# Broadcast loads of 1/den in a linear-attention block: 128 partitions in rows of 2 KB in place of 32 partitions in rows of 8 KB

## Chip, cores and metric

The kernel runs on one core of a Trainium2 chip. The metric is the device time of one execution in microseconds (us), lower is better. The core has five engines that the program gives separate instruction streams: PE (TensorE, matrix multiply), ACT (ScalarE), DVE (VectorE), POOL (GpSimd) and SP (SyncE). SP does no arithmetic here; it issues nearly all of the kernel's DMAs, in program order, and 16 DMA engines carry them out. A DMA tells of its landing by raising a semaphore by 16.

## Reference

One block of a conditioned transformer, all inputs and the output in bf16: S = 2048 tokens of width D = 1024, 32 attention heads of width 32, a feed-forward layer of width F = 3584.

```
mod = (silu(c) @ w_mod)                      # six vectors: sa, ca, ga, sb, cb, gb
h   = layernorm(x) * (1 + ca) + sa
q, k, v = heads of (h @ wqkv)
pq, pk  = phi(q), phi(k)                     # phi(t) = (t + 1 if t > 0 else exp(t)) + 1e-6
kv  = sum over s of pk[s, d] * v[s, e]       # per head
z   = sum over s of pk[s, d]
num = pq @ kv
den = (pq . z) + 1e-6                        # one number per head and token
x   = x + ga * ((num / den) @ wo)
h   = layernorm(x) * (1 + cb) + sb
x   = x + gb * ((gelu(h @ w_gate) * (h @ w_up)) @ w_down)
```

The part that matters here is the division by den.

## The kernel before

The kernel has one program, written out by a Python planner: every operation is recorded with the bytes it reads and writes, from which the waits follow, and each engine's stream is then emitted in the recorded order. In one stretch (from `mark[0]`, L1050, to L1765) a list scheduler, `reorder`, moves the DVE, ACT and POOL operations by estimated costs and due times; PE and SP keep the recorded order there. The loads of 1/den for token blocks 0 to 2, and the scaling of block 0 and of half of block 2, are recorded in that stretch, the rest behind it.

**Tiling.** Tokens are 16 chunks of 128 (`c_`), or 4 blocks of 512 (`sg`, 0 to 3), each block in two halves of `HW` = 256 tokens (`h`). The 32 heads are 8 groups (`g`, `NG` = 8) of 4 (`k`, `HPG` = 4); a group's 4 heads of width 32 fill the 128 partitions, so head k of a group lies in partitions 32k to 32k+31. `PQ[sg]` holds phi(q) as [128 partitions, 8 groups, 512 tokens].

**The path of 1/den.** `den` (L1235) makes the denominators of two blocks on PE (128 rows: block, half, head k, group g; 256 tokens along the row), takes their reciprocal on DVE and stores the 128 rows of 1 KB in DRAM, in `scr_rd[sg, h, k, g, t]` (L1248). `rb_load(sg, hs)` (L1255) brings them back, each head's values copied into the 32 partitions of that head: `RB[i]`, i = sg % 2, is [128, 2 halves, 8 groups, 256 tokens] in f32. For each block and half it issues four loads of 256 KB on SP's queue, one per head k: 32 partitions, each the same row of 8 KB. There are 32 such loads. `pq_scale(sg, h, gs)` (L1268) then multiplies phi(q) by RB on DVE, in four instructions per block and half, each over two head groups [128 x 512]; each of these waits for all four loads of its block and half (`rb_ops`).

**What uses it.** `wo_mm` (L1278) multiplies the scaled `PQ[sg]` of one chunk of 128 tokens by `W2` (K-V state times output weights) on PE, 16 matrix multiplies per chunk, and DVE adds the result to x (`x1`, L1291). A chunk can only be finished when both its block's half has been scaled and W2 is there.

**Order.** Around the change SP issues, in this order: the store of den 0; a transposing DMA `mT4` (L703); the 8 loads of block 0; `mT5` (PE needs it for `kv_prod(5)`, L913); the store of den 1; `mT6`; a small store of `mrg`; `mT7`; 16 loads (block 2 half 0, block 1 halves 0 and 1, block 2 half 1); then, between transposing DMAs `T2` of the second layer norm (`h2a`, `h2b`), loads of x and the first feed-forward weights `wt`, four loads for block 3 half 0 and four for half 1. Transfers on SP's queue take eight semaphores in turn ("lanes"): before SP issues a DMA, the DMA issued eight earlier must have landed. DVE and PE too run strictly in their order. Behind L1765 the chunks 3 to 13 of `wo_mm` come one after another, with the `pq_scale` of later blocks recorded between them (`SLOT`, L1769), and then the feed-forward layer: unit 0 (with chunks 14 and 15 inside it), and 27 more.

Of the kernel before, what the change touches and what calls it, by code (L numbers as in the profile page):

```python
# [10 lines left out]
P = 128  # L11
# [7 lines left out]
NG = 8  # L19
HPG = 4  # L20
# [310 lines left out]
def bass_adaLN_cond__linear_attn_block__geglu_ffn__prompt_kernel(  # L331
# [17 lines left out]
    scr_rd = nc.dram_tensor("scr_rd", [NSG, 2, HPG, NG, SGW // 2], f32).ap()  # L349
    with ExitStack() as es:  # L350
# [6 lines left out]
        def at(name, shape, dty, off):  # L357
            return nc.alloc_sbuf_tensor_at(name, shape, dty, offset=ABASE + off, align_bytes=4)
# [39 lines left out]
        RB = [at(f"rb{i}", [P, 2, NG, SGW // 2], f32, OFF_RB[i]) for i in range(2)]  # L398
# [46 lines left out]
        def r_sm(name):  # L445
            return [(SMO[name], SMO[name] + SMSZ[name], name)]
# [30 lines left out]
        def r_wv(g):  # L477
            return [(OFF_WK + g * 2048, OFF_WK + (g + 1) * 2048, "wv")]
# [4 lines left out]
        def r_pq(sg, k0=0, k1=NG, s0=0, s1=SGW):  # L483
            return r_t8(PQO[sg], f"pq{sg}", k0, k1, s0, s1)
# [46 lines left out]
        def r_rb(i, h, g0=0, g1=NG):  # L531
            return [(OFF_RB[i] + (h * NG + g0) * 1024, OFF_RB[i] + (h * NG + g1) * 1024, f"rb{i}")]
# [10 lines left out]
        def pr(b):  # L543
            return [(b * 2048, (b + 1) * 2048)]
# [7 lines left out]
        sch = Sched()  # L552
        T, A, V, G, Q = PE_, ACT_, DVE_, POOL_, SP_
# [64 lines left out]
        for q in range(1, 4):  # L618
            wmq_dma(q)
            for d0, d1 in ((2 * q, 2 * q + 1), (2 * q + 1, 2 * q + 2)):  # L620
# [8 lines left out]
               rd=r_sm("c8") + r_sm("ident"), pwr=pr(4))  # L629
# [4 lines left out]
               rd=r_sm("thc") + r_sm("chalf"), wr=r_sm("siluT"))  # L634
# [507 lines left out]
        for c_ in range(10, NCH):  # L1142
            b = seq.index(("k", c_ // 2 * 2, 0)) - (9 if c_ % 2 else 12)
# [6 lines left out]
        for c_ in range(8, NCH, 2):  # L1150
            b = seq.index(("k", c_, 0)) - 3
# [10 lines left out]
        for g in range(NG):  # L1162
            task(nk + g // 2, lambda g=g: sch.dma(Q, lambda e: e.dma_start(WV[:, g, :, :], wqkv_v[:, :, 2 * D + g * P:2 * D + (g + 1) * P]),
                                                  wr=r_wv(g), note=f"wv{g}"))
# [68 lines left out]
        HW = SGW // 2  # L1233
# [16 lines left out]
            return store  # L1250

        o_rd = {}
        rb_ops = {}

        def rb_load(sg, hs=(0, 1)):  # L1255
            i = sg % 2
            for h in hs:
                made = []
                for k in range(HPG):
                    made.append(sch.dma(Q, lambda e, h=h, k=k: e.dma_start(  # L1260
                        RB[i][32 * k:32 * (k + 1), h, :, :].rearrange("p a b -> p (a b)"),
                        scr_rd[sg, h, k:k + 1, :, :].rearrange("k g t -> k (g t)").to_broadcast([32, NG * HW])),
                        wr=r_rb(i, h) if k == 0 else (), deps=made[0].deps if k else [o_rd[sg // 2]], note=f"rb{sg}.{h}.{k}"))
                rb_ops[sg, h] = made

        GH = [((0, 2), (2, 4)), ((4, 6), (6, 8))]

        def pq_scale(sg, h, gs):  # L1268
            i, t0 = sg % 2, h * HW
            for g0, g1 in gs:  # L1270
                ap = PQ[sg][:, g0:g1, t0:t0 + HW]
                rng = r_pq(sg, g0, g1, t0, t0 + HW)
                sch.op(V, lambda e, ap=ap, i=i, h=h, g0=g0, g1=g1: e.tensor_tensor(ap, ap, RB[i][:, h, g0:g1, :], ALU.mult),
                       rd=rng + r_rb(i, h, g0, g1), wr=rng, deps=rb_ops[sg, h], note=f"pqs{sg}.{h}.{g0}")

        x1_ops, s_ops = {}, {}

# [28 lines left out]
        def hook_run(f):  # L1306
            if f[:2] == "kv":
                kv_prod(int(f[2:]), 4)
            elif f == "ga":
                ga_pass()  # L1310
            elif f == "gbr":
                assert mdone[0] == 64
                gb_rows()
            elif f == "modp":
                mod_pass()
            elif f == "z32":
                z32()
            elif f[:3] == "den":
                st[int(f[3:])] = den(int(f[3:]), 5)
                st[int(f[3:])]()  # L1320
            elif f[:2] == "ps":
                pq_scale(int(f[2]), int(f[4]), GH[0] + GH[1])
            elif f[:2] == "rb":
                rb_load(int(f[2]), (int(f[4]),))
            elif f[0] == "w":
                w2_pair(int(f[1:]))
# [27 lines left out]
        kv_prod(7, 5)  # L1354
        wo_mm(0, 0, [4, 5])
        rb_load(1)
        rb_load(2, (1,))
        w2_pair(3)
        wo_mm(1, 2, [3, 4, 5])
# [229 lines left out]
        def down(c_, k, b, c0, c1, fcs, last, after):  # L1589
# [5 lines left out]
            if last:  # L1595
                pset_writer(b, o)

        pq_scale(2, 0, GH[0] + GH[1])

        def r_wh(q, r, cc, name, j0, j1):  # L1600
# [165 lines left out]
        def cb1():  # L1766
            sch.op(V, lambda e: e.tensor_scalar(CB1T[:, :], CBT[:, :], 1.0, None, op0=ALU.add), rd=r_sm("cbT"), wr=r_sm("cb1T"))

        SLOT = {2: lambda: (pq_scale(1, 0, GH[0] + GH[1]), x_dma(NXR, 10)),  # L1769
                3: lambda: pq_scale(1, 1, GH[0] + GH[1]),  # L1770
                4: lambda: (cb1(), wt_dma(0)),
# [54 lines left out]
        for n in range(12):  # L1826
            q, i = divmod(n, 4)
# [6 lines left out]
        for u in range(2 * NFP):  # L1834
# [5 lines left out]
            else:  # L1840
                a = ACTS.get(u, ((), ()))
# [143 lines left out]
```

## Time and profile before

| | |
|---|---|
| times of three runs | 782.70, 782.91, 783.98 us; median 782.91 |
| profiled execution | span 780.9 us from its first to its last instruction; the profile gives no total of its own for what lies around the span |
| PE | 770.2 us busy, 99% of the span |
| DVE, ACT, POOL | 83%, 48%, 6% of the span |
| granted TensorE clock | 1.000 |
| DMA packets | 196940, 130.22 MB |
| loads of 1/den | 32 of 256 KB, issued from 176.7 to 236.4 us; median 6.0 us from issue to landing |
| scaling by 1/den on DVE | 32 instructions, 684 ns each, from 185.6 to 247.7 us |

PE's share of busy time is that of pipelined matrix multiplies, so 99% says that PE rarely waits, not that it runs at its peak. The trace also keeps a record for every DMA packet (size, start, duration) and one for every rise of a DMA semaphore. From these come the durations of single packets and the landing times of single DMAs that the prediction uses.

### The profile page before, as it was taken

How to read it: one execution, taken by the hardware profiler on the slowest of the kernel's cores; microseconds unless marked ns; L12 is line 12 of the kernel's file. 1: busy time of each engine (PE TensorE's matmuls, PEld its weight loads, DVE VectorE, ACT ScalarE, POOL GpSimd, SP SyncE). 2: the span in 40 equal slices, each digit the busy share in tenths (PEclk: the TensorE clock that was granted, in tenths of full speed). 3: DMA queues.
4: the chain of work that ended last, by engine and by line, in shares of the span. 5: the costliest groups of instructions: out<-in, count | busy, mean ns of one | idle time of the engine just before them, and what ended most of it. 6: DMA issues, size and time to landing. Idle time of an engine off the chain costs nothing.

```text
span 780.9 us, 10753 instructions
## 1 busy us (share of the span) xinstructions
PE 770.2 (99%) x3825; PEld 496.2 (64%) x3883; DVE 645.9 (83%) x964; ACT 374.6 (48%) x629; POOL 47.5 (6%) x126
## 2 busy tenths in 40 slices
PE   8999999999999999999999999999999999999998
PEld 4444445666445667667676767667676576677766
DVE  6699988897899878787989888888989888676767
ACT  2497743242466487878755555555555211111111
POOL 2031300000321011100000000000000000000000
PEclk9999999999999999999999999999999999999999
DMA  9879749939999358867353865535356334443331
GB/s 284 256 167 252 158 91 215 255 80 196 203 287 231 82 138 212 230 175 215 99 145 108 250 211 172 148 96 161 97 147 221 111 127 139 144 141 114 126 125 60
DMA packets 196940, 130.22 MB, mean 167 GB/s; under 512 B 69516, under 2 KB 182420, under 8 KB 195864
## 3 DMA queue, kind: packets, MB, share of 16 engines
q1 hardware_dynamic: 196872, 129.55, 62.4%
q8 instruction: 30, 0.49, 0.3%
q14 instruction: 22, 0.18, 0.1%
q10 hardware_dynamic: 16, 0.00, 0.0%
HBM read 92.55 MB, written 23.35 MB: 148 GB/s over the span
## 4 chain that ended last, share of the span: by engine, by line
PE 95%; SPq 2%; DMA 1%; DVE 1%; issue 1%; ACT 0%; DVEq 0%; ACTq 0%
PE ps_all L1458 45%; PE ps_all L1672 21%; PE ps_all L895 7%; PE ps_all L934 7%; PE ps_all L1283 7%; PE ps_all L880 5%; PE ps_all L1593 1%; SPq L598 1%; DMA wmq<-in_w_mod_dram 1%; SPq L603 1%; DMA h1T<-xh 0%; PE ps_all L913 0%; PE ps_all L1201 0%; PE ps_all L1240 0%; DVE h1T L724 0%
## 5 line engine op out<-in xcount | busy, mean ns | idle before, releaser
L1458 PE MATMUL ps_all<-ss,tp 128*128 128x512 f32 x896 | 214.3, 396 | 0.0
L1458 PEld LDWEIGHTS ps_all<-ss,tp 128*128 128x128 f32 x896 | 168.3, 188 | 37.8 <-DVE ss L1413 0.2
L1672 PE MATMUL ps_all<-dt,sb 128*128 128x512 f32 x424 | 102.5, 398 | 0.0
L1481 ACT ACTIVATE ge<-ps_all 128x512 f32<-128x512 f32 x112 | 64.1, 597 | 73.8 <-DVE ps_all L1469 62.1
L1458 PE MATMUL ps_all<-h2a,wt 128*128 128x512 bf16 x421 | 95.7, 379 | 1.8
L1672 PEld LDWEIGHTS ps_all<-dt,sb 128*128 128x128 f32 x424 | 79.6, 188 | 18.5 <-DVE sb L1648 0.3
L1476 DVE TENSOR_TENSOR ps_all<-ps_all,es 128x512 f32<-128x512 f32 x54 | 37.6, 699 | 49.4 <-ACT es L1466 49.0
L1488 DVE TENSOR_TENSOR ys<-ge,ps_all 128x512 bf16<-128x512 f32 x112 | 74.4, 684 | 3.8 <-PE ps_all L1672 0.5
L1458 PEld LDWEIGHTS ps_all<-h2a,wt 128*128 128x128 bf16 x448 | 38.0, 98 | 57.3 <-ACT ps_all L1463 16.9
L1433 DVE TENSOR_TENSOR tp<-wt 128x1024 fp32r<-128x1024 bf16 x56 | 68.1, 1217 | 1.8 <-DMA wt<-in_B_w_up_dram 1.8
L1433 DVE TENSOR_TENSOR tp<-wt,tp 128x1024 fp32r<-128x1024 bf16 x56 | 68.2, 1218 | 0.0
L934 PE MATMUL ps_all<-h1T,wq 128*128 128x512 bf16 x256 | 56.7, 379 | 0.0
L880 PE MATMUL ps_all<-wk,h1T 128*128 128x512 bf16 x239 | 55.3, 379 | 1.1 <-DMA wk<-in_A_wqkv_dram 0.5
L1283 PE MATMUL ps_all<-w,pq 128*128 128x512 bf16 x249 | 55.7, 379 | 0.5 <-issue 0.2
L1458 PE MATMUL ps_all<-ar,tp 128*128 128x512 f32 x224 | 55.5, 390 | 0.0
L869 ACT ACTIVATE eb<-ps_all 128x512 f32<-128x512 f32 x64 | 36.3, 594 | 37.6 <-PE ps_all L880 16.0
L1672 PE MATMUL ps_all<-wd,ya 128*128 128x512 bf16 x199 | 47.5, 380 | 0.7
L1458 PEld LDWEIGHTS ps_all<-ar,tp 128*128 128x128 f32 x224 | 42.1, 188 | 8.9
L1463 ACT ACTIVATE ps_all<-ps_all 128x512 f32<-128x512 f32 x56 | 32.6, 582 | 26.8 <-PE ps_all L1458 26.5
L934 PEld LDWEIGHTS ps_all<-h1T,wq 128*128 128x128 bf16 x256 | 25.0, 98 | 30.0
L1283 PEld LDWEIGHTS ps_all<-w,pq 128*128 128x128 bf16 x256 | 24.6, 98 | 30.3 <-issue 1.1
L1643 ACT ACTIVATE sb<-ya 128x896 fp32r<-128x896 bf16 (+1 forms) x16 | 14.5, 913 | 58.8 <-PE ps_all L1672 58.8
(141 smaller groups left out, 976.3 us busy)
## 6 DMA issues: line engine op xcount, KB each, us to landing
wt<-in_B_w_gate_dram SPq DMA_DIRECT2D x28, 512.0 KB, 4.0
wt<-in_B_w_up_dram SPq DMA_DIRECT2D x28, 512.0 KB, 5.2
scr_y<-ys SPq DMA_DIRECT2D x28, 512.0 KB, 3.2
ya<-scr_y SPq DMA_DIRECT2D x14, 896.0 KB, 4.9
rb<-scr_rd SPq DMA_DIRECT2D x32, 256.0 KB, 6.0
wd<-in_B_w_down_dram SPq DMA_DIRECT2D x7, 1024.0 KB, 7.6
wmst<-in_w_mod_dram SPq DMA_DIRECT2D x6, 1024.0 KB, 6.2
wmq<-in_w_mod_dram SPq DMA_DIRECT2D x8, 512.0 KB, 7.5
```

The lines of the kernel that those rows point to most:

```text
L869: sch.op(A, lambda e: e.activation(EB[i][:, :], PS(bank), ACTF.Exp), prd=pr(bank), wr=rng, note=f"{note}.exp")
L880: o = sch.op(T, lambda e, dc=dc: e.matmul(PS(bank), H1[sg][:, ci, dc, :], W_[:, dc, jg * 512:(jg + 1) * 512], start=(dc == 0), stop=(dc == ...
L895: o = sch.op(T, lambda e, c_=c_: e.matmul(PS(bank, 0, n), PK[c_][:, g * P:(g + 1) * P], xrow(c_, o_, o_ + n), start=(c_ == 0), stop=(c_ == ...
L934: o = sch.op(T, lambda e, dc=dc: e.matmul(PS(b), WQ[:, dc, qc * P:(qc + 1) * P], H1[sg][:, :, dc, :], start=(dc == 0), stop=(dc == NDC - 1 ...
L1283: last[half] = sch.op(T, lambda e, g=g, half=half: e.matmul(PS(b0 + half), PQ[sg][:, g, ci * P:(ci + 1) * P], W2[:, g, half * 512:(half + ...
L1433: sch.op(V, lambda e: e.tensor_tensor(TP[k][:], in0, in1 if k in (0, 2) else in1[:], ALU.subtract), rd=r0 + r1, wr=r_tp(k), deps=[x1_ops[7 ...
L1458: o = sch.op(T, lambda e, l_=l_, r_=r_, dc=dc: e.matmul(PS(b), l_, r_, start=fresh and dc == 0, stop=dc == ND2 - 1, skip_group_check=True) ...
L1463: sch.op(A, lambda e: e.activation(PS(BB + t), PS(BA + t), ACTF.Copy), prd=pr(BA + t), pwr=pr(BB + t), note="pcp")
L1476: sch.op(V, lambda e: e.tensor_tensor(PS(BC + t), PS(BC + t), ES[t][:, :], ALU.add), prd=pr(BC + t), rd=r_2k(OFF_ES[t], f"es{t}"), pwr=pr( ...
L1481: sch.op(A, lambda e: e.activation(GE[i][:, :], PS(b), ACTF.Gelu_apprx_tanh), prd=pr(b), wr=r_2k(OFF_GE[i], f"ge{i}"), note="gelu")
L1488: sch.op(V, lambda e: e.tensor_tensor(YS[s_][:, 2 * h:2 * h + 2, t, :], q(GE[i][:, :]), q(PS(b + 1)), ALU.mult), rd=r_2k(OFF_GE[i], f"ge{i ...
L1672: o = sch.op(T, lambda e, l_=l_, r_=r_, j=j, dst=dst: e.matmul(dst, l_[:, 0, :], r_, start=(k in (1, 5) or own is not None) and j == js[0] ...
```

## The change

The four loads of a block and half are cut the other way. Before, one load brought one head k: all 8 groups (a row of 8 KB) to that head's 32 partitions. After, one load brings two head groups g0 and g0+1 for all four heads: a row of 2 KB (2 groups x 256 tokens x 4 bytes) to each of the 128 partitions. The destination is [128 partitions, 512 elements]; the source is described as [4 heads, 32 copies with step 0, 512 elements]. The number of loads (32), the bytes of each (256 KB), their queue and their place in the order stay. Each scaling instruction of `pq_scale`, which covers two head groups, now waits for the one load that brought them, where it waited for four; and each load waits for the readers of its own two groups' bytes rather than the first load for those of the whole half.

```
         def rb_load(sg, hs=(0, 1)):
             i = sg % 2
             for h in hs:
-                made = []
-                for k in range(HPG):
-                    made.append(sch.dma(Q, lambda e, h=h, k=k: e.dma_start(
-                        RB[i][32 * k:32 * (k + 1), h, :, :].rearrange("p a b -> p (a b)"),
-                        scr_rd[sg, h, k:k + 1, :, :].rearrange("k g t -> k (g t)").to_broadcast([32, NG * HW])),
-                        wr=r_rb(i, h) if k == 0 else (), deps=made[0].deps if k else [o_rd[sg // 2]], note=f"rb{sg}.{h}.{k}"))
-                rb_ops[sg, h] = made
+                for g0 in range(0, NG, 2):
+                    src = scr_rd[sg, h, :, g0:g0 + 2, :].rearrange("k g t -> k (g t)").unsqueeze(1).to_broadcast([HPG, P // HPG, 2 * HW])
+                    sch.dma(Q, lambda e, h=h, g0=g0, src=src: e.dma_start(
+                        RB[i][:, h, g0:g0 + 2, :].rearrange("p a b -> p (a b)"), src),
+                        wr=r_rb(i, h, g0, g0 + 2), deps=[o_rd[sg // 2]], note=f"rb{sg}.{h}.{g0}")
...
                 sch.op(V, lambda e, ap=ap, i=i, h=h, g0=g0, g1=g1: e.tensor_tensor(ap, ap, RB[i][:, h, g0:g1, :], ALU.mult),
-                       rd=rng + r_rb(i, h, g0, g1), wr=rng, deps=rb_ops[sg, h], note=f"pqs{sg}.{h}.{g0}")
+                       rd=rng + r_rb(i, h, g0, g1), wr=rng, note=f"pqs{sg}.{h}.{g0}")
```

## The prediction

> **What bounds the kernel now.** I read the page's chain of waits first, for what sets the end.
>
> ```profile
> PE 95%; SPq 2%; DMA 1%; DVE 1%; issue 1%; ACT 0%; DVEq 0%; ACTq 0%
> ```
>
> PE is 95% of the chain, so a change to DMAs can gain only where PE waits today, and lose wherever it makes PE wait. Next the table of windows over the stage that the loads lie in (columns: stretch, its length, then busy time and instructions of PE, PEld, DVE, ACT, POOL, the granted clock, the busy share of the 16 DMA engines, GB/s).
>
> ```profile
> 165.00:177.00 12.00, 12.00 (x121) 7.35 (x120) 10.15 (x15) 4.98 (x10) 0.00 (x0) 1.00 0.43 107
> 177.00:190.00 13.00, 13.00 (x126) 8.52 (x125) 9.83 (x16) 3.29 (x7) 0.00 (x0) 1.00 1.15 215
> 190.00:207.00 17.00, 16.79 (x108) 8.01 (x108) 11.98 (x23) 4.88 (x7) 1.65 (x5) 1.00 0.93 201
> 207.00:222.00 15.00, 14.89 (x69) 6.78 (x70) 14.19 (x29) 11.22 (x14) 9.10 (x21) 1.00 1.08 235
> 222.00:242.00 20.00, 19.89 (x92) 9.07 (x93) 17.70 (x32) 13.31 (x23) 3.38 (x8) 1.00 1.11 246
> 242.00:262.00 20.00, 19.95 (x90) 11.86 (x89) 19.41 (x26) 8.98 (x13) 1.47 (x3) 1.00 0.55 151
> ```
>
> Two things are to be seen. PE is busy in 96.53 of 97.00 us, so the whole stage has 0.47 us to give. And the DMA engines' share is near or over 1 from 177 to 242 us: the queue is full, just fast enough. Third, the loads themselves (the view of tile rb):
>
> ```profile
> L1260 SPq DMA_DIRECT2D rb<-scr_rd x32: 302/419/1351, 176.7 to 236.4; - x32
>   DMA rb<-scr_rd: 2.2, 2
> DMA to landing us min/median/max: 3.6/6.0/10.5
> ```
>
> DVE waited 2.2 us for them, twice; PE next to nothing. Last, SP's order of issue (start, duration, engine, line):
>
> ```profile
> 176.69 3.76 SPq L1260 DMA_DIRECT2D rb<-scr_rd  x8
> 180.55 1.23 SPq L703 DMA_TRANSPOSE mtb<-mb  x1
> 185.74 0.35 SPq L1248 DMA_DIRECT2D scr_rd<-rdc  x1
> ...
> 192.51 12.38 SPq L1260 DMA_DIRECT2D rb<-scr_rd  x16
> ...
> 222.33 1.92 SPq L1260 DMA_DIRECT2D rb<-scr_rd  x4
> ...
> 233.97 2.86 SPq L1260 DMA_DIRECT2D rb<-scr_rd  x4
> ```
>
> Behind every burst of loads stand DMAs that PE needs soon: `mT5` for `kv_prod(5)`, the store of den 1, the `T2` transposes, `wt`.
>
> **What a load costs now.** In the semaphore records the 8 loads of the first burst land at 180.26, 181.50, 182.67 and so on to 188.62: one every 1.2 us. The packet records say why: each engine carries two rows of 8 KB, and an 8 KB packet takes 602 ns in these bursts, against 309 ns where it has its way to itself. So two engines share one way into the 32 partitions. The loads of `wo`, 2 KB rows into 64 partitions, show the same: 152 to 159 ns a packet, against 84 ns for the 2 KB rows of x into 128 partitions. Thus 64 neighbouring partitions have no more ways than 32.
>
> **How many engines carry a load after the change.** This decides everything. The traces show that a DMA doesn't always use 16 engines:
>
> ```profile
> q10 hardware_dynamic: 16, 0.00, 0.0%
> ```
>
> q10 carried one DMA, the load of c in 8 rows of 256 bytes, and left 16 packets: 8 of data and 8 of 4 bytes that raise the semaphore, where 16 engines would leave 16 of those. Its semaphore rose in 9 steps (8 engines, and the rest at once); the stores of `mrow` (4 rows) rose in 5 steps; loads with 32 or 128 rows in 16. So the number of engines follows the count of the outermost dimension. The new load has 128 at its destination, but its source is 4 heads x 32 copies x 512 elements: outermost 4. No DMA of this trace has two sides that differ like this. I take it that the smaller side decides: 4 engines with 32 rows each. [...]
>
> **The price of a load.** With 4 engines each has 32 rows of 2 KB. Low: 84 ns a row (x) gives 2.7 us. High: 155 ns (`wo`), if two of the engines stand at one way all the time: if each engine takes 32 neighbouring partitions, the first two go through partitions 0 to 63, which share their ways by the rows above, and so do the other two. That is 5.0 us. They share only while they are in step, and the engines of one DMA land up to 0.3 us apart (x), which is more than three rows of 84 ns, so neither row is nearer: I take the middle, 120 ns and 3.8 us. It stands against 1.2 us now: +2.6 us a load (bounds +1.5 and +3.8).
>
> **Part by part.**
> 1. 32 loads, +2.6 us each, on engines that all the other DMAs need too (a transposing DMA or a weight load lands when its last engine is done): +84 us (bounds +48, +122) until the last load of block 3 has landed. The queue has no idle time to absorb it (shares above). The gap while the store of den 1 lands and its first dependent load starts stays as it is.
> 2. How it reaches PE. First `mT5`: it landed at 189.58, PE used it at 190.42, 0.84 us of slack. It stands behind 8 loads: 8 x 2.6 = 21, so PE first stops some 20 us at L913. The den 1 store stands behind the same loads, so the 16 loads that wait for it start as much later, and take 42 us more. In DVE's order `pq_scale(2, 1)` stands behind x1 of chunk 5, and x1 of chunks 6 and 7 behind it; so do the transposes made from them. Then 8 loads of block 3: +21. These stalls don't add to the 84; they are its pieces.
> 3. Slack at the end: the last load landed at 242.37, its scaling began at 245.94 because DVE was busy: 3.6 us. The matrix multiplies of chunk 14 and unit 0 (L1458) wait for that scaling and for `s_sum` behind it on DVE. Shift: 84 - 3.6 = 80 us.
> 4. Scaling waits for one load instead of four: worth up to three loads' time on the first of four instructions, nothing on the last, which the chunk needs. Nothing, because it is the fourth that PE waits for.
> 5. Issue: 0.42 us of SP a load now; `gab` (128 rows) took 0.35. Same. The lane waits grow, but SP waits for what the engines would make it wait for anyway.
> 6. The scheduler may place a DVE operation otherwise, as a scaling is ready sooner in its plan: bounds one cast of 1.2 us either way; I take nothing. Behind 262 us nothing changes: the feed-forward layer starts late and runs the same.
>
> Sum: 780.9 + 80 = 861 for the profiled execution's span. The median of the runs is 2.0 above that span: 863 us. With the bounds of point 1: 827 to 901.
>
> **Rivals.**
> *A, all 16 engines carry the new load (not slower).* Each then has 8 rows at 84 ns: 0.67 us in place of 1.2, and 32 x 0.5 = 17 us of queue time come free. For it: the load of `gab`, a copy of one row to 128 partitions, ran on 16 engines at 159 ns for 4 KB; but its source is described with 128 copies outermost. Against it: the 9 and 5 steps. It would gain at most PE's idle 0.47 us: 782.4 to 782.9, and the place where it shows is the scaling's wait of 2.2 us on DVE, gone. It decides from the point at which a load takes less than 1.2 + 3.6/32 = 1.3 us, that is 8 engines at 84 ns. [...]
> *B, 4 engines, and all four at the same way at all times (slower still).* If rows are dealt out one by one, four neighbouring rows go to four engines at once. Two engines share a way at 8 KB in 602 ns each, so a 2 KB row among four takes 301 ns, a load 9.6 us: 32 x 8.4 - 3.6 = 265, some 1048 us. Nothing in the trace shows such dealing: in the 32-row loads, rows dealt by turns would have put four engines on one way, at 1.2 us a packet, and they show 602 ns.
>
> **How the numbers follow.** Forecast (4 engines, 84 to 155 ns a row) 0.83, A 0.12, B 0.05. Point: the likeliest's, 863. Range 815 to 905: the forecast's bounds with some room for a queue that is less full than I read it; it leaves out A, B and a few hundredths. 0.2% (1.6 us) is about what a measurement can tell from no change. A gives same, and faster only if the stage gives more than its visible idle time: faster 0.03, same 0.10, slower 0.87.
>
> **What would show it.** In the profile after: q1's mean share of 16 engines low in the stage (some 0.4 where it was 1.1) while loads take over 10 us to land; landings 2.7 to 5.0 us apart; fewer completion packets (32 x 12 = 384 less); PE idle at L913 for some 20 us, with mtb as its releaser, then at L1283 on pq, and DVE's waits for rb in tens of us. Landings 0.7 us apart would show A; 16 steps of the semaphore would too. The forecast is wrong if the source's outermost 4 doesn't limit the engines, and its size is wrong if the rows take other than 120 ns.

## The result, and the profile after

The kernel after takes 831.38 us (median of 4 runs, 830.91 to 834.20) against 782.81 us before (782.31 to 783.98): a ratio of 1.0624, 95% interval 1.0606 to 1.0642, or 48.6 us more. The profiled execution has a span of 830.0 us, 49.1 more than before.

The page's chain of waits, the line that showed PE at 95%:

```profile
PE 82%; SPq 8%; DMA 7%; DVE 2%; issue 1%; DVEq 0%
```

SP's queue and the DMAs now hold 15% of the way to the end, where they held 3%. The table of windows over the stage, which has grown by some 48 us (columns as before):

```profile
177.00:190.00 13.00, 11.44 (x114) 7.46 (x113) 8.74 (x13) 3.01 (x7) 0.00 (x0) 1.00 0.29 91
190.00:210.00 20.00, 9.89 (x61) 4.82 (x59) 5.13 (x8) 1.93 (x3) 0.00 (x0) 0.74 0.72 114
210.00:230.00 20.00, 16.49 (x79) 6.51 (x76) 10.33 (x18) 6.90 (x9) 2.83 (x9) 0.91 0.26 100
230.00:250.00 20.00, 15.70 (x64) 6.44 (x65) 8.98 (x15) 2.37 (x3) 2.85 (x9) 0.91 0.72 106
250.00:270.00 20.00, 14.45 (x61) 5.91 (x60) 12.05 (x27) 11.66 (x15) 4.60 (x14) 0.90 1.10 184
```

Where only loads of 1/den run (177 to 190, 210 to 230), the mean share of the 16 DMA engines is 0.26 to 0.29, where it was near 1: about 4 engines work and 12 stand idle, while PE has lost up to half of a window. The third-last column, the granted clock, which was 1.00 in every window, falls to 0.74 where PE stopped longest. Who PE waited for, and the loads' own view:

```profile
PE ps_all L1280 <- DVE pq L1270: 14.7, 9, 4.6
PE ps_all L913 <- DMA mtb<-mb: 10.1, 1, 10.1
...
PE ps_all L840 <- DVE rdc L1245: 1.6, 1, 1.6
```

```profile
L1259 SPq DMA_DIRECT2D rb<-scr_rd x32: 504/868/4408, 177.5 to 280.7; - x32
L1270 DVE TENSOR_TENSOR pq<-pq,rb x32: 627/692/723, 183.8 to 295.4; 128x512 bf16<-128x512 bf16 x32
its engine sat idle before it (us, times) until:
  DMA rb<-scr_rd: 42.4, 26
```

PE stops once for 10.1 us at `kv_prod(5)`, behind the first burst, and then again and again for scaled `PQ`; DVE's wait for the loads is 42.4 us in 26 pieces, where it was 2.2 us in 2. SP's order of issue from the first burst to the store of den 1:

```profile
177.53 13.09 SPq L1259 DMA_DIRECT2D rb<-scr_rd  x8
190.73 7.37 SPq L703 DMA_TRANSPOSE mtb<-mb  x1
198.20 0.53 SPq L1248 DMA_DIRECT2D scr_rd<-rdc  x1
```

The 8 issues that took 3.76 us take 13.09, and the store of den 1 goes out 12.5 us later. Two counts settle how many engines carry a load. In the semaphore records each of the 32 loads now rises in 5 steps, which is what the 4-row stores did: 4 engines and the rest at once. And the page counts

```profile
DMA packets 199628, 130.22 MB, mean 157 GB/s; under 512 B 69132, under 2 KB 182036, under 8 KB 199576
```

2688 packets more than before: 32 x 96 = 3072 more rows of data, and 32 x 12 = 384 fewer completion packets. The rows themselves run at 84 ns (median of the 2 KB packets from 177 to 290 us), so a load takes 32 x 84 ns = 2.7 us by its packets, and lands every 2.6 us.

The landing times, from the semaphore records (us from the start of each span):

```
                                     before    after    difference
first load of block 0                180.26   183.74      3.5
last load of block 0                 188.62   201.93     13.3
transposing DMA mT5                  189.58   202.78     13.2
first of the 16 (block 2 half 0)     196.09   211.38     15.3
last of the 16                       215.11   251.11     36.0
block 3 half 0, first and last       226.09   265.32     39.2
                                     229.65   273.00     43.4
block 3 half 1, first and last       238.76   285.03     46.3
                                     242.37   295.36     53.0
scaling of block 3 half 1 done       248.43   296.07     47.6
```

The delay grows in every burst and between them too, but for 0.1 us at `mT5`. At the last load it is 53.0 us; 32 x 1.40 (2.60 against 1.20 us between landings) makes 44.8 of it.

### The profile page after: what moved, and what is told of

The parts are those of the page before. It is cut to its first block, busy times and chain, and to the rows that moved or that the text cites. A ratio compares the mean times of both kernels' runs of the same rounds, so it can differ in the third digit from the quotient of the medians.

```text
span 830.0 us, 10807 instructions
## 1 busy us (share of the span) xinstructions
PE 787.8 (95%) x3883; PEld 499.0 (60%) x3883; DVE 647.7 (78%) x964; ACT 374.3 (45%) x629; POOL 44.1 (5%) x126
## 4 chain that ended last, share of the span: by engine, by line
PE 82%; SPq 8%; DMA 7%; DVE 2%; issue 1%; DVEq 0%
PE ps_all L1455 42%; PE ps_all L1669 20%; PE ps_all L934 7%; PE ps_all L880 6%; PE ps_all L895 5%; SPq L1259 4%; DMA rb<-scr_rd 4%; SPq L703 2%; DMA mtb<-mb 1%; PE ps_all L1590 1%; DMA wmq<-in_w_mod_dram 1%; SPq L598 1%; SPq L603 0%; PE ps_all L1280 0%; DVE xall L1288 0%
## 5 line engine op out<-in xcount | busy, mean ns | idle before, releaser
L1455 PE MATMUL ps_all<-ss,tp 128*128 128x512 f32 x896 | 216.8, 399 | 2.4 <-DVE ss L1410 2.4
L1455 PE MATMUL ps_all<-h2a,wt 128*128 128x512 bf16 x448 | 102.4, 381 | 4.8 <-ACT ps_all L1460 2.6
L1280 PE MATMUL ps_all<-w,pq 128*128 128x512 bf16 x256 | 65.9, 415 | 15.7 <-DVE pq L1270 14.7
L1270 DVE TENSOR_TENSOR pq<-pq,rb 128x512 bf16<-128x512 bf16 x32 | 22.0, 691 | 42.4 <-DMA rb<-scr_rd 42.4
```

The source lines that it names most:

```text
L1280: last[half] = sch.op(T, lambda e, g=g, half=half: e.matmul(PS(b0 + half), PQ[sg][:, g, ci * P:(ci + 1) * P], W2[:, g, half * 512:(half + ...
L1455: o = sch.op(T, lambda e, l_=l_, r_=r_, dc=dc: e.matmul(PS(b), l_, r_, start=fresh and dc == 0, stop=dc == ND2 - 1, skip_group_check=True) ...
```

## The experiments

**The number of engines: three kernels.** `e1_copies4` and `e2_copies2` store den several times in DRAM, so that the source has 16 or 8 entries outermost; the loads' rows, partitions and bytes are those of the kernel after.

```
-    scr_rd = nc.dram_tensor("scr_rd", [NSG, 2, HPG, NG, SGW // 2], f32).ap()
+    scr_rd = nc.dram_tensor("scr_rd", [NSG, 2, HPG, 4, NG, SGW // 2], f32).ap()
...
-                o_rd[pr_] = sch.dma(Q, lambda e: e.dma_start(scr_rd[2 * pr_:2 * pr_ + 2].rearrange("s f k g t -> (s f k g) t"), RDC[:, :]),
+                o_rd[pr_] = [sch.dma(Q, lambda e, r=r: e.dma_start(scr_rd[2 * pr_:2 * pr_ + 2, :, :, r].rearrange("s f k g t -> (s f k) g t"), RDC[:, :]),
...
-                    src = scr_rd[sg, h, :, g0:g0 + 2, :].rearrange("k g t -> k (g t)").unsqueeze(1).to_broadcast([HPG, P // HPG, 2 * HW])
+                    src = scr_rd[sg, h, :, :, g0:g0 + 2, :].rearrange("k r g t -> (k r) (g t)").unsqueeze(1).to_broadcast([HPG * 4, P // HPG // 4, 2 * HW])
```

> The kernel after, but den is stored four times in DRAM (four stores of 128 KB in place of one), so that the source of a load has 16 entries outermost (4 heads x 4 copies, each read 8 times) and not 4. Rows, partitions, bytes and number of loads are those of the kernel after. Theory (the smaller of the two outermost counts sets the number of engines, and that alone made the kernel slow): 16 engines a load, 17 semaphore steps at most, loads land about 0.7 us apart instead of 2.6, PE waits for nothing in the stage, 782 to 785 us; the three more stores may cost up to 2 us at the first burst, which has slack. Rival (rows of 2 KB into 128 partitions, read many times from one place in DRAM, are slow whatever the number of engines): landings stay over 1.2 us apart and the time over 795 us.

Measured: 783.57 us against 782.54 (ratio 1.0013, interval 1.0004 to 1.0021). The semaphores rise in 16 steps, and the loads land 0.86 to 1.13 us apart (the means of the four bursts). The view of tile rb:

```profile
L1259 SPq DMA_DIRECT2D rb<-scr_rd x32: 514/594/856, 179.4 to 235.6; - x32
its engine sat idle before it (us, times) until:
  DMA rb<-scr_rd: 1.3, 3
...
DMA to landing us min/median/max: 4.0/5.4/6.8
```

The 42.4 us of DVE's waits are 1.3, below the 2.2 of the kernel before. So rows of 2 KB into 128 partitions are quick when 16 engines carry them, and all but 1.0 of the 48.6 us is gone. Each stored row is also read 8 times here and not 32, as it lies in DRAM four times; `e7_before4` below, where every row is still read 32 times, tells that apart from the number of engines.

> As e1_copies4 with two copies: 8 entries outermost. Theory: 8 engines with 16 rows of 84 ns each, landings 1.3 us apart (9 semaphore steps), near the break-even of 1.3 us: +0.14 us x 32 = 4.5 us of queue time, less about 4 us of slack at the end: 783 to 787 us. If the count of engines fell to 4 unless it is 16, the time would be that of the kernel after, 831 us.

Measured: 793.06 us (ratio 1.0131, 1.0115 to 1.0146): 9 steps, so 8 engines, as the theory says, but over the 783 to 787 that it gave. The loads landed 1.75, 1.40, 1.81 and 2.73 us apart in the four bursts, not 1.34; in the first burst the median packet took 104 ns (186 to 200 us), where 84 was reckoned. The profiled execution was the slowest of the four, 796.50 us. PE's waits (sum, times, longest):

```profile
PE ps_all L913 <- DMA mtb<-mb: 5.8, 1, 5.8
PE ps_all L1455 <- ACT ps_all L1460: 2.7, 1, 2.7
```

`mT5` is late again, by less. The reckoning with 84 ns a row fits most landings of the second burst, which are 1.3 us apart, and failed in the other bursts: in the first, a row took 104 ns in the median with 8 engines and 84 with 4 (the kernel after, 178 to 202 us). Why is not shown.

`e7_before4` takes the other side: the kernel before, with only the description of the source changed.

```
-                        scr_rd[sg, h, k:k + 1, :, :].rearrange("k g t -> k (g t)").to_broadcast([32, NG * HW])),
+                        scr_rd[sg, h, k:k + 1, :, :].rearrange("k g t -> k (g t)").unsqueeze(1).to_broadcast([4, 8, NG * HW])),
```

> The kernel before, with its loads as they are (32 partitions, rows of 8 KB, scalings wait for all four), but the source of each described as 4 x 8 copies of the row in place of 32 copies: the same bytes to the same places. Theory (outermost 4 means 4 engines): each engine has 8 rows of 8 KB at 309 ns when it shares its way with nobody, 2.5 us a load against 1.2 now: 32 x 1.3 = 42, with the starts of the bursts and less the slack some +40 to +50: 823 to 835 us. Rival (the shape of the rows and the 128 partitions did it): no change, 782 to 784 us.

Measured: 826.70 us (ratio 1.0563, 1.0549 to 1.0578). The same bytes go from and to the same places in rows of 8 KB; the semaphores rise in 5 steps, the packets take 309 ns instead of some 600, and the loads of the first burst land 2.47 us apart. Its page has 196556 packets, 384 fewer than before: only completions are gone. Without any of the new shape, and with each row read 32 times as before, the description alone costs 44.2 us, against the 48.6 of the whole change. So the loads whose source has 4, 8 and 16 entries outermost raise their semaphores in 5, 9 and 16 steps (`e7_before4`, `e2_copies2`, `e1_copies4`).

**Which burst costs what.** `e4_block0` and `e5_block3` are the kernel before with the new loads for one block.

```
             for h in hs:
                 made = []
+                if sg in (0,):        # (3,) in e5_block3
+                    rb_ops[sg, h] = []
+                    for g0 in range(0, NG, 2):
...
+                    continue
                 for k in range(HPG):
```

> The kernel before, with only the 8 loads of block 0 cut the new way (4 engines each). Theory (one queue carries everything, and PE has 0.84 us of slack at the transposing DMA mT5 behind the first burst): mT5 lands some 13 us later as in the kernel after, PE stops 10 to 12 us at L913, and as PE is busy without a gap behind it nothing of that is made up: 792 to 795 us. Rival (only the queue's delay at the last load counts, less the 5 us of slack there): 788 to 790 us.

> The kernel before, with only the 8 loads of block 3 cut the new way. In the kernel after, the two bursts of block 3 made the queue 17 us later: 8 x 1.39 = 11.1 by the packets' own time, the rest at the start of each burst and, in the last one, while x, gbb and wt run ahead on the other 12 engines. Theory (that rest belongs to these bursts, and some 5 us of slack at the last scaling comes off): 793 to 796 us. Rival (packets' own time alone): 11.1 less 5, 788 to 790 us. If PE had not been waiting on this burst at all: 783 us.

Measured: 796.13 us for block 0 and 796.17 for block 3, each 13.0 over the 783.16 of the kernel before (ratios 1.0164, 1.0150 to 1.0178, and 1.0162, 1.0146 to 1.0178). Both are just over the upper end of what the theory gave and well above the rival's 788 to 790. In `e4_block0` the cost is one stop, and behind it the loads run at the old 1.2 to 1.3 us again while PE never catches up:

```profile
PE ps_all L913 <- DMA mtb<-mb: 10.1, 1, 10.1
PE ps_all L840 <- DVE rdc L1245: 1.4, 1, 1.4
```

In `e5_block3` everything is as before to 222 us, and PE then waits in small pieces around the start of the feed-forward layer:

```profile
PE ps_all L1466 <- ACT ps_all L1471: 2.6, 1, 2.6
PE ps_all L1466 <- DVE ss L1421: 2.4, 1, 2.4
PE ps_all L1291 <- DVE pq L1281: 2.4, 2, 1.4
PE ps_all L1466 <- DVE xall L1299: 2.2, 1, 2.2
```

So 8 such loads cost 13 us in both places, more than the 8 x 1.4 = 11.2 of their packets. That it is the same is chance: the parts differ, and one of them is the granted clock, which neither expectation had. PE's order around the stop, in the kernel before and then in `e4_block0`:

```profile
190.42 0.61 PE L913 MATMUL ps_all<-mtb,wv 128*128 128x128 bf16 x8
197.21 44.41 PE L1283 MATMUL ps_all<-w,pq 128*128 128x512 bf16 x201 [0.16 <-issue]
```

```profile
201.49 1.01 PE L913 MATMUL ps_all<-mtb,wv 128*128 128x128 bf16 x8 [10.07 <-DMA mtb<-mb]
210.81 44.41 PE L1291 MATMUL ps_all<-w,pq 128*128 128x512 bf16 x201 [0.16 <-issue]
```

`mT5` lands 11.8 us later, and PE goes on 11.1 us later: about the delay less the 0.84 us of slack. The long run of `wo_mm` starts 13.6 us later, and by 13.6 us the span has grown. The 2.5 us between are matrix multiplies at half the clock: its records show 0.5 from 196.6 to 206.8 us, and the eight of L913 take 1.01 us where they took 0.61. In `e5_block3` the last load lands 17.1 us later and its scaling is done 11.8 us later; behind it, eight matrix multiplies of unit 0 take 3.65 us where they took 2.11, with the clock at 0.5 from 263.9 to 267.4 us, and the span is 13.2 us longer.

In the queue itself, the starts of the bursts cost more than the packets' usual time: in the kernel after, the 2 KB packets that started from 208 to 210 us, as the second burst began, took 119 ns in the median and 202 at the 95th percentile, those from 212 to 216 us 84. In the last burst the loads land 3.4 us apart while x, gbb and wt go ahead on the other 12 engines: the semaphore of the load of x behind them rises 12 times from 287.97 to 289.97 us and 4 times from 296.13 to 296.70.

**Do PE's stops add up?** `e10_after_spread` is the kernel after with the second four loads of block 0 behind `mT5`.

```
-        HOOK = {..., 17: "w1 rb0.0 rb0.1", ..., 19: "kv4", ...}
+        HOOK = {..., 17: "w1 rb0.0", ..., 19: "kv4 rb0.1", ...}
```

> The kernel after (4 engines), with the second four loads of block 0 issued behind the transposing DMA mT5. PE's first stop at L913, 10.1 us in the kernel after, must shrink to 0 to 3 us, as mT5 stands behind four loads instead of eight. Theory of the prediction (the queue sets the pace, PE's stops are pieces of its delay and don't add): PE stops later instead, where it waits for mT6 behind the same 8 loads, and the time stays within 2 us of 831. Rival (the stop at L913 is a loss of its own): 821 to 824 us.

Measured: 830.26 us (ratio 1.0610, 1.0594 to 1.0626), against 831.38 for the kernel after. PE's waits:

```profile
PE ps_all L1280 <- DVE pq L1270: 15.4, 9, 4.1
PE ps_all L913 <- DMA mtb<-mb: 3.7, 3, 2.0
PE ps_all L1201 <- DVE kvt L920: 2.9, 1, 2.9
```

The stop of 10.1 us has shrunk to 3.7 in three pieces: 1.3 for `mT5`, 2.0 for `mT6` and 0.4 for `mT7`. A wait of 2.9 us at L1201 is new. The long run of `wo_mm` starts 3.0 us earlier than in the kernel after (208.81 against 211.81 us) and then waits for scaled `PQ` all the same; the last load lands 1.9 us earlier, and the time is the same within the intervals. So the queue sets the pace, and most of a stop that is taken away comes back behind the same loads.

**The waits.** `e3_allwaits` is the kernel after, with each scaling waiting for all four loads again.

```
+                made = rb_ops[sg, h] = []
...
-                       rd=rng + r_rb(i, h, g0, g1), wr=rng, note=f"pqs{sg}.{h}.{g0}")
+                       rd=rng + r_rb(i, h, g0, g1), wr=rng, deps=rb_ops[sg, h], note=f"pqs{sg}.{h}.{g0}")
```

> The kernel after, but each scaling instruction waits for all four loads of its half again. Theory of the prediction (the finer wait is worth nothing, PE waits for the fourth load anyway): 831 to 832 us. Rival (with loads 2.6 us apart the first three scalings are done before the fourth load lands, so the coarse wait puts three more scalings of 0.6 us behind the last load, which is on the path): +1.8 us at the end, 833 to 834 us.

Measured: 830.36 us (ratio 1.0615, 1.0596 to 1.0634), the same as after within the intervals. The finer wait brings nothing that the time shows. The rival's cost is there all the same: with the coarse wait the last scaling is done 2.6 us after the last landing, in the kernel after 0.7. But the last load of `e3_allwaits` landed 2.5 us earlier (292.81 against 295.36 us), which makes up for it; why it did stays open.

**Fewer, larger loads.** `e6_rows8k` is the kernel after with one load of 1 MB for each half.

```
-                for g0 in range(0, NG, 2):
-                    src = scr_rd[sg, h, :, g0:g0 + 2, :].rearrange("k g t -> k (g t)").unsqueeze(1).to_broadcast([HPG, P // HPG, 2 * HW])
+                for g0 in (0,):
+                    src = scr_rd[sg, h].rearrange("k g t -> k (g t)").unsqueeze(1).to_broadcast([HPG, P // HPG, NG * HW])
```

> The kernel after, with one load of 1 MB for each block and half in place of four (128 partitions, rows of 8 KB, source 4 x 32 copies, so 4 engines of 32 rows); each scaling waits for the whole load. 8 loads in place of 32, the same bytes. Theory (the bytes on 4 engines set the time): 32 rows x 309 ns = 9.9 us a load, 2.5 for each 256 KB, near that of e7_before4: 822 to 830 us. Rival (what matters is SP, which in the kernel after needs 2.4 us for an issue as soon as four loads are outstanding): with 8 issues that is gone, and the time is below 815 us.

Measured: 851.12 us (ratio 1.0860, 1.0840 to 1.0880). Both expectations missed. The loads of the second burst land 9.9 us apart, as 32 rows of 309 ns ask, but DVE waits longer, for whole loads, and PE with it:

```profile
PE ps_all L1280 <- DVE pq L1270: 27.5, 4, 17.1
PE ps_all L840 <- DVE rdc L1245: 11.9, 1, 11.9
PE ps_all L1280 <- DVE w L1208: 10.4, 1, 10.4
```

In DVE's order the work on den 1 stands behind scalings that wait for 1 MB: PE waits 11.9 us at L840 for its first step, and the store of den 1 goes out at 207.32 us, where it went at 198.20 in the kernel after. The loads of block 0 have all landed by 204.92 us, and the next ones are issued from 211.20 us on. The time is not below 815 us, as the rival had it; but SP is still held, 9.99 us at one load and 13.0 to 16.6 us at DMAs behind loads, so this kernel doesn't test SP alone.

**The last microsecond with 16 engines.** `e1_copies4` is 1.0 us over the kernel before. Two kernels looked for it: `e8_copies4_allwaits` (the coarse waits of `e3_allwaits` in `e1_copies4`) and `e9_spread`, whose edit is in the order of SP:

```
-        HOOK = {..., 16: "den0", 17: "w1 rb0.0 rb0.1", ..., 19: "kv4", ...}
+        HOOK = {..., 16: "den0", 17: "st0 w1 rb0.0", ..., 19: "kv4 rb0.1", ...}    # den0: one store; st0: the other three
```

> e1_copies4 (16 engines), but each scaling waits for all four loads of its half, with which the planner again puts the reciprocal of den 1 ahead of the scalings of block 0 on DVE, as in the kernel before. Theory (the 1.0 us that e1_copies4 is over the kernel before comes from the order of DVE: two scalings that wait for DMAs stand ahead of that reciprocal): 782.3 to 783.0 us, PE without a gap from 177 to 190 us. Rival (it comes from the three more stores of den): 783.4 to 783.8 us as in e1_copies4.

> e1_copies4 (16 engines, four copies of den) with SP's order mended at the first burst: one of the four stores of den 0 ahead of the transposing DMA mT4, three behind it, and of the 8 loads of block 0 the second four behind mT5. In e1_copies4 and e8_copies4_allwaits PE was idle 0.9 to 1.0 us at L913, because mT4 stood behind four stores and landed at 180.3 in place of 178.4. Theory (that gap is their +0.9 to +1.0 us): gone, 782.3 to 783.0 us when the kernel before is at 782.5 to 783.2, so no difference to it; PE has only 0.5 us to give in this stage, so no gain either. Rival (the stores cost elsewhere): still 0.8 to 1.2 us over the kernel before.

Measured: 784.05 us against 783.16 (ratio 1.0014, 1.0005 to 1.0023) and 784.40 against 782.69 (ratio 1.0022, 1.0013 to 1.0030). Both theories fall: neither order brings the microsecond back. The windows show how PE's gap moved. First `e8_copies4_allwaits`, then `e9_spread`:

```profile
177.00:190.00 13.00, 12.10 (x119) 7.74 (x118) 9.40 (x15) 3.12 (x7) 0.00 (x0) 1.00 0.90 244
190.00:207.00 17.00, 16.79 (x109) 8.19 (x110) 10.84 (x21) 4.88 (x7) 0.94 (x3) 1.00 0.90 248
```

```profile
177.00:190.00 13.00, 13.00 (x127) 8.52 (x126) 8.18 (x13) 2.83 (x6) 0.00 (x0) 1.00 0.83 204
190.00:207.00 17.00, 15.80 (x100) 7.31 (x101) 13.09 (x24) 4.87 (x7) 0.94 (x3) 1.00 1.01 257
```

In the first, PE idles 0.9 us before 190 us: `mT4` stands behind four stores of den 0 and lands at 179.93 us, before at 178.42. With these moved, PE idles 1.0 us after 190 us, at L913, for `mT6` behind the stores of den 1: it lands at 194.76 us, before at 191.99. So the extra stores seem to delay whichever transposing DMA stands behind them. The profiled execution of `e9_spread` was the fastest of eleven, 783.48 us and 0.8 over the kernel before; why the median is 1.7 over stays open. No version tried here beats the kernel before.

## Why the prediction was right, and where it was not

- **The deciding step**, that the source's outermost 4 leaves 4 engines, was the author's assumption and held: 5 steps, 384 fewer completions, a share of 0.26 to 0.29 (it named some 0.4). `e1_copies4` and `e7_before4` show from both sides that this is the cause: 16 engines take away all but 1.0 us, and 4 engines without the new shape cost 44.2. Rival A's condition was made in `e1_copies4` and gave nearly what A reckoned: 783.57 against its 782.4 to 782.9, no difference over 0.2%, with landings 0.9 to 1.1 us apart instead of 0.7. Rival B found nothing: the rows ran at 84 ns.
- **The size failed in one term**, the price of a load: 120 ns a row and 3.8 us, the middle between the rows of x (84) and of `wo` (155). Measured: 84 ns and 2.6 us between landings. The point of 863 was therefore 32 us too high. The high bound rested on engines that share a way, the author's inference from rows that took about twice the time (602 ns against 309, 155 against 84); which engines do, no run shows. In the kernel after the rows took 84 ns in the median, and more only at the starts of bursts (119 from 208 to 210 us) and in the last one (116 from 285 to 290 us). The row of the same shape, 2 KB into 128 partitions, was the one to take. With it the prediction's own sum was 827, its lower bound; 831 was measured. That they are so near is in part luck, as the delay and the slack were both larger than that sum has them (below). Three readings were rough: the loads of x spread over 0.1 to 3.0 us between their first and last engine, where 0.3 is that of the early ones; the 8 KB packets took some 606 ns in the median, not 602; and the 4 KB packets of `gab` 180, 159 being the commonest. Only the first bears on the price, as a reason for the middle.
- **The queue term** (32 times the excess of a load) was +84 with bounds +48 and +122; the last load landed 53.0 us later. 44.8 are the loads' own; the other 8 had no term. A first issue 0.8 us later, slow packets at the starts and the last burst's crowding are among them; they were not measured apart.
- **How it reaches PE**: the stop at L913 was put at 20 us and was 10.1, first by the same mis-sized price. `mT5` landed 13.2 us later, 11.2 of it by the loads; the slack took 0.84 off, and PE itself came to L913 2.2 us later than before, 1.6 of it by a wait at L840. That PE's stops are pieces of the queue's delay and don't add, `e10_after_spread` shows. The slack at the end, named as 3.6 us, was 53.0 - 47.6 = 5.4: the other three scalings were done while the last load was still on its way.
- **"Behind 262 us nothing changes"** was nearly right: from the first DVE instruction behind the last scaling to the end it was 532.6 us and is 534.0, 1.4 us more. The granted clock is the reason that the trace shows: it is 0.5 from 300.0 to 303.4 us, and eight matrix multiplies there take 3.49 us where they took 2.11.
- **The finer wait is worth nothing**: held for the time (`e3_allwaits`), but not for the reason given. On the last four scalings it is worth the three that need not stand behind the last landing, 1.9 us, and in `e3_allwaits` an earlier last landing hides that.
- **Issue, "same"**: wrong. An issue takes 0.50 us and more, and from the fifth load in flight on SP is held some 2.5 us for each. It cost little: in `e7_before4` SP issues a load in some 0.6 us, and the loss is only 4.4 us less, of which 32 x 0.13 = 4.2 go with landings 2.47 us apart instead of 2.60.
- **The scheduler**, put at nothing within 1.2 us: it did place two scalings, which wait for DMAs, ahead of the reciprocal of den 1, and PE waits 1.6 us at L840 for it. In `e3_allwaits`, where the old order is back, that wait is gone, the stop at L913 is 11.3 us, and the time is within the intervals of the kernel after's: the wait shows no cost of its own.

## What to carry to other kernels

Before reshaping a DMA, look at the outermost count of both sides, the broadcast source included: it can take 16 engines down to 4 (here 16 steps down to 5, and 384 fewer completion packets), and the steps in which a landing DMA raises its semaphore, or the number of completion packets, tell how many there are. A DMA that is slower on a full queue costs first at whatever stands behind it, and moving that out of its way only moves the stop (in `e10_after_spread` the stop of 10.1 us became 3.7, and the time 830.26 us against 831.38); reckon the delay of the queue as a whole and subtract the slack once, at the last place where PE waits for it (0.84 us at `mT5` in `e4_block0`, 5.4 at the last scaling in `e5_block3` and in the kernel after). Then add what the lowered clock costs PE behind that last stop, 1.4 to 2.5 us here. Where a price lies between two rows of the trace, take the row with the same row size and the same partitions, not the middle; with 8 engines (`e2_copies2`) even that was too low, 84 ns against 104 in the first burst.

## What the runs showed of the hardware that was not expected

- Packets can be slow as a burst begins and quicker behind it. In `e6_rows8k` the packets of 8 KB that started from 176 to 186 us took 606 ns in the median, those from 186 to 200 us 315; in the kernel after, the 2 KB packets are slow only at the starts of bursts (119 ns in the median from 208 to 210 us, 84 from 212 to 216) and in the last burst, beside x, gbb and wt (116 ns in the median from 285 to 290 us). The cause is not shown.
- SP is held when much is outstanding: with 32 rows an engine the fifth load's issue and each later one take some 2.5 us, about a load's time on its engines; with 8 rows an engine (`e7_before4`) 8 issues go out in 5.29 us. What holds SP, no run settles.
- The granted clock falls while PE waits: 0.74 from 190 to 210 us, around the 10.1 us stop, and a mean of 0.981 over the execution; the mean matrix multiply of `wo_mm` went from 379 to 415 ns. In the kernel after, most of that fell where PE went on to wait for the queue anyway, and 1.4 us shows at the end; in `e4_block0`, where nothing makes PE wait again, it cost 2.5 of 13.6 us. The clock's records come in pieces of 3.41 us or a multiple of it. Reckoned from PE's instructions, the kernel after has the clock at 0.5 behind each piece in which PE idled 2.0 us or more, and a clock of 1.00 stays so behind those with up to 1.7. Two stops of 1.5 us, at 237.4 and 240.0 us, put 2.0 us of idle time into one piece, and the clock is 0.5 from 241.9 to 245.4 us.
